# RetNet recurrence and RWKV channel mix on one core: 64-token chunks from block 2 on, four early loads, key weights in quarters, a new order

## The chip, the cores and the metric

The kernel runs on one core of one Trainium2 chip. The metric is the device time of one execution in microseconds, as the median of several runs. A profile of one execution stands beside it; its span runs from the first to the last instruction of the program.

## The reference, cut to what matters

Two layers follow each other. The first is a linear attention with decay (8 heads of 64, 4 sequences of 768 tokens); the second mixes channels (model width 512, hidden width 1024) and looks one token back.

```
state = gamma[h] * state + k_t (outer) v_t          # per head, 64 x 64
y_t   = scale * q_t @ state
x  = y, heads side by side: (4, 768, 512)
xk = mu_k * x + (1 - mu_k) * x_prev;   xr = mu_r * x + (1 - mu_r) * x_prev
k  = relu(xk @ w_k);   v = (k * k) @ w_v;   r = sigmoid(xr @ w_r)
out = r * v
```

## The kernel before, in words

**Blocks.** The 4 x 768 tokens are cut into 12 blocks n = 0..11 of 256 tokens; three blocks make a sequence, and the state is carried from block to block of one sequence. Each block goes through attention pieces and then through three projections (keys, gates, values). GROUPS joins blocks 3 and 4, 6 and 7, 9 and 10 for the keys.

**The order is written out by hand.** ORDER (line 24 on) is a list of words; the kernel is recorded word by word, so each engine runs its own words in exactly this sequence. A word such as `S.6@45` is a code, its block (and further numbers) and the PSUM banks that it uses; `~v`, `~a`, `~p`, `~s` name VectorE (DVE), ScalarE (ACT), GpSimd (POOL) and SyncE (SP). An engine that waits at a word holds back all of its later words. The codes:

- `lq`, `lk`, `lv`: loads of q, k, v of a block (line 222). Most go through GpSimd's queue and turn f32 to f16 on the way for q and k. `wk`, `wr`, `wv`: the weights (lines 733 to 742), on the same queue. `mu`: the two mixing vectors, on ScalarE's queue.
- EARLY (line 18) names loads that land as f32 in a scratch area and are cast by `cq` and `ck` (line 245). Before, these are the first halves (heads 0 to 3) of block 0's q and k, on SyncE's queue.
- `Tq`, `Tk`: transposes on TensorE (line 264); `Eq`, `Ek`: their copies out of PSUM by ScalarE (lines 285, 297). Blocks in WHOLE turn 128 tokens at a time, the others 64.
- `vs`: v times decay (line 252). `S`: scores k by q (lines 312, 324); `M`: the causal mask on their way out of PSUM (line 345). `C`: products of k and v for the state (lines 359, 373), `U`: sums of these into the carried states (line 406), `G`: their decay to the next block (line 421).
- `I`: the part of y that comes from the carried states, for half of the tiles (line 450); `Y`: the part within the chunk, and in most blocks the other half of the carried part (line 470); `J`: that other half alone, where Y lacks it (line 453). `D`: y out of PSUM into x (line 501).
- `dx`, `t`, `X`: the difference to the token before and the two mixes (lines 525, 539, 547); `X.n.0.*` feed the keys, `X.n.1.*` the gates. `K`, `R`, `V`: the projections (lines 567, 608, 622), `Qa` and `Qb` relu and square, `s` the sigmoid, `O` the product, `st` the store.
- `z.c`: matmuls of zeros in spare time (line 700); `mt`, `me`: the mixing vectors turned; `gy`, `cm`: tables made at the start.

**Three kinds of attention.** HALF blocks (6 to 11) cut a block into four chunks of 64 tokens; every matmul is a 64x64 tile with 64 columns, the mask is one instruction of 128x1024, and there are four states to sum (`U.n.0` to `U.n.3`, three in the last block of a sequence). `D` is then two instructions. WIDE blocks (2 to 5) have two chunks of 128 tokens: scores as 64x128 tiles, two masks of 128x1024, two sums (one in the last block of a sequence), one `D`. Blocks 0 and 1 interleave even and odd tokens.

**Start.** constants() (line 662) loads the small tables on ScalarE's queue, clears a few tiles, and applies one Sigmoid to a dummy tile, which makes ScalarE load its function table.

Of the kernel before, what the change touches and what calls it, by code (L numbers as in the profile page):

```python
# [799 lines left out]
```

## Time and profile before

| | |
|---|---|
| median of 3 runs | 153.58 us (153.42 to 153.73) |
| span of the profiled execution | 151.4 us, 2.2 us under that median |
| TensorE (PE) busy | 143.4 us, 2426 matmuls |
| VectorE (DVE) busy | 127.8 us, 212 instructions |
| ScalarE (ACT) busy | 103.6 us, 195 instructions |
| GpSimd (POOL) busy | 55.3 us |
| granted TensorE clock | full throughout |

In a timeline, the columns are the start in us, the time from the start of the first to the end of the last instruction of the merged row, engine, line, operation, tiles (out<-in), shapes and count. Matmuls overlap each other, so what a piece costs on a busy TensorE is read from start to start. PEld is the loading of weights, which runs beside PE. In a group row, "17.9, 577" is the busy time of the group in us and the mean duration of one instruction in ns.

### The profile page before, as it was taken

What the parts mean: (1) busy time and instruction counts of PE and PEld (TensorE: products, weight loads), DVE (VectorE), ACT (ScalarE), POOL (GpSimd) and SP (SyncE); (2) the same over time, 40 slices, a digit from 0 to 9 for tenths busy, and PEclk for the clock granted to TensorE, in tenths of its full rate; (3) what the DMA queues carried; (4) which work ended last, traced back from release to release, by engine and by line L of the source; (5) the groups of instructions that cost most, each with busy time, mean ns of one, the idle gap of its engine ahead of it and who ended that gap; (6) DMA issues with size and microseconds to landing.
All of it is one profiled execution on the core that took longest, in us unless ns stands there. A gap on an engine that the chain in (4) does not pass through costs nothing.

```text
span 151.4 us, 5541 instructions
## 1 busy us (share of the span) xinstructions
PE 143.4 (95%) x2426; PEld 82.8 (55%) x2426; DVE 127.8 (84%) x212; ACT 103.6 (68%) x195; POOL 55.3 (37%) x65
## 2 busy tenths in 40 slices
...
GB/s 140 219 229 197 207 231 192 168 251 212 196 167 202 233 262 107 256 300 198 231 173 126 7 38 283 105 35 45 0 4 0 4 0 211 205 0 0 148 133 139
DMA packets 45624, 22.16 MB, mean 146 GB/s; under 512 B 37400, under 2 KB 41248, under 8 KB 45600
## 3 DMA queue, kind: packets, MB, share of 16 engines
...
q8 instruction: 19, 0.31, 0.8%
q10 hardware_dynamic: 304, 0.18, 0.4%
...
## 4 chain that ended last, share of the span: by engine, by line
PE 73%; DMA 12%; POOL 11%; issue 1%; DVE 0%; POOLq 0%
PE ps L624 27%; PE ps L572 14%; DMA v<-in_v_dram 12%; PE ps L612 12%; PE ps L582 8%; PE ps L278 3%; POOL q L235 3%; POOL k L230 2%; PE ps L441 2%; POOL vs L253 2%; POOL v L230 2%; PE ps L366 1%; PE ps L462 1%; PE ps L642 1%; PE ps L318 1%
## 5 line engine op out<-in xcount | busy, mean ns | idle before, releaser
L624 PE MATMUL ps<-wv,k2s 128*128 128x512 f16 x184 | 44.1, 380 | 0.0
L591 ACT ACTIVATE kr<-ps 128x512 f32<-128x512 f32 x48 | 27.9, 594 | 12.5 <-PE ps L582 6.5
L624 PEld LDWEIGHTS <-k2s 128*128 128x128 f16 x184 | 17.1, 98 | 18.9 <-ACT k2s L603 0.4
L630 DVE SCALAR_TENSOR_TENSOR os<-ps,rs 128x512 f32<-128x512 f32 x23 | 15.6, 684 | 11.9 <-ACT rs L618 9.4
L612 PE MATMUL ps<-wr,xr 128*128 128x512 f16 x96 | 23.5, 379 | 0.0
L582 PE MATMUL ps<-xk,wk 128*128 128x256 f16 x192 | 23.2, 273 | 0.0
L572 PE MATMUL ps<-xk,wk 128*128 128x512 f16 x96 | 23.0, 379 | 0.0
L618 ACT ACTIVATE rs<-ps 128x512 f32<-128x512 f32 x24 | 13.6, 597 | 12.9 <-PE ps L612 12.1
L230 POOL DMA_DIRECT2D k<-in_k_dram x20 | 17.8, 903 | 10.3 <-PE ps L384 6.7
L582 PEld LDWEIGHTS <-wk 128*128 128x128 f16 x192 | 18.1, 98 | 3.7
L241 ACT COPY qT<-ps 128x1024 f16<-128x1024 f16 (+1 forms) x13 | 12.3, 946 | 9.5 <-PE ps L278 7.8
L558 DVE SCALAR_TENSOR_TENSOR xr<-dx,mu,xT 128x256 f16<-128x256 f32 (+1 forms) x32 | 17.9, 577 | 0.1
L230 POOL DMA_DIRECT2D v<-in_v_dram x18 | 16.0, 911 | 3.6 <-DMA wr<-in_moe_w_r_dram 1.9
L558 DVE SCALAR_TENSOR_TENSOR xk<-dx,mu,xT 128x256 f16<-128x256 f32 (+1 forms) x32 | 17.0, 579 | 0.2
L354 DVE TENSOR_TENSOR a<-ps,c_sb 128x1024 f16<-128x1024 f32 (+1 forms) x14 | 14.6, 1066 | 0.9 <-PE ps L339 0.6
L603 ACT ACTIVATE k2s<-kr 128x512 f16<-128x512 f32 x24 | 14.8, 631 | 0.3
L612 PEld LDWEIGHTS <-xr 128*128 128x128 f16 x96 | 9.0, 97 | 10.7 <-issue 0.5
L572 PEld LDWEIGHTS <-wk 128*128 128x128 f16 x96 | 9.1, 98 | 10.5
L599 ACT ACTIVATE k2s<-kr 128x512 f16<-128x512 f32 x24 | 14.5, 627 | 0.3
L241 ACT COPY kT<-ps 128x1024 f16<-128x1024 f16 (+1 forms) x13 | 12.2, 945 | 2.2 <-PE ps L272 1.7
L529 DVE TENSOR_TENSOR dx<-xT 128x1024 f32<-128x1024 f32 x11 | 13.4, 1221 | 0.2
L253 DVE TENSOR_TENSOR vs<-v,csm_sb 128x1024 f16<-128x1024 f32 x10 | 12.2, 1217 | 0.2 <-DMA v<-in_v_dram 0.2
...
## 6 DMA issues: line engine op xcount, KB each, us to landing
out_dram<-os SPq DMA_DIRECT2D x23, 256.0 KB, 2.4
v<-in_v_dram POOLq DMA_DIRECT2D x18, 256.0 KB, 7.7
q<-in_q_dram POOLq DMA_DIRECT2D x11, 256.0 KB, 8.4
...
```

Of the source, the lines that this page charges most:

```text
L230: e.dma_start(out=dst[:, :, i * D : i * D + D], in_=src[:, i * P : i * P + P].rearrange("h p d -> p h d"),)
L241: e.copy(out=out, in_=in_)
L253: e.tensor_tensor(out=VS(n), in0=V32(n).rearrange("p h (i d) -> p i h d", i=2), in1=gks[:, int(half(n) or wide(n)), :, :, None].to_broadca ...
L354: nc.vector.tensor_tensor(out=a_full(n)[:, i, :, j0:j1], in0=pairs(banks("S", n, i, j0))[:, :, j0:j1], in1=(below if wide(n) else causal[: ...
L558: nc.vector.scalar_tensor_tensor(out=XM[w](k)[:, j, t0:t1], in0=DX(k)[:, j, t0:t1], scalar=mu[:, w * NCO + j : w * NCO + j + 1], in1=x[:, ...
L572: nc.tensor.matmul(banks("K", n, g), lhsT=wk16[:, co, g * P : g * P + P], rhs=XM[0](k)[:, co, :], start=(co == 0), stop=(co == NCO - 1),)
L582: nc.tensor.matmul(pz[:, i, :], lhsT=wk16[:, co, fo * P : fo * P + P], rhs=XM[0](k)[:, co, m * TM + t0 : m * TM + t1], start=(i == 0 and c ...
L591: nc.scalar.activation(out=kr, in_=banks("K", n, g, *u), func=AF.Relu)
L603: nc.scalar.activation(out=K2(n)[:, w * g : w * g + w, t0:t1], in_=kr.rearrange("p a t -> p (a t)").rearrange("p (i t) -> p i t", i=w), fu ...
L612: nc.tensor.matmul(banks("R", n, tb), lhsT=XM[1](k)[:, co, t : t + P], rhs=wr16[:, co, :], start=(co == 0), stop=(co == NCO - 1),)
L624: nc.tensor.matmul(banks("V", n, tb), lhsT=K2(n)[:, fo, tb * P : tb * P + P], rhs=wv16[:, fo, :], start=(fo == 0), stop=(fo == NFO - 1),)
L630: nc.vector.scalar_tensor_tensor(out=OS(2 * n + tb), in0=banks("V", n, tb), scalar=1.0 / (KSC * KSC), in1=RS(2 * n + tb), op0=ALU.mult, op ...
```

## The change

The blocks 2 to 5 become HALF blocks, and blocks 2 and 3 leave WHOLE. The second halves of block 0's q and k are loaded as f32 on ScalarE's queue and cast by VectorE (`cq.0.2.4~v`, `ck.0.2.4~v`). The key weights come in four loads of 256 columns. A new piece `w.n~a` (fence) stands behind each `I.n`: ScalarE reads one column per tile of the PSUM banks that I.n wrote, so that Y.n, which writes to the same banks, waits for it. The Sigmoid on the dummy tile becomes a word of its own, `wm~a`, in the middle of block 0's work; in the built program ScalarE has a second table load at that place, beside one ahead of its first cast. The scaling `vs.3` goes from GpSimd to VectorE, and all pieces stand in a new order. What is cut from the two orders below lies behind the first key projection of blocks 6 and 7.

```diff
-HALF = (6, 7, 8, 9, 10, 11)
-EARLY = ((1, 0, 0), (0, 0, 0))
+HALF = (2, 3, 4, 5, 6, 7, 8, 9, 10, 11)
+EARLY = ((0, 0, 0), (1, 0, 0), (0, 0, 2), (1, 0, 2))
-WHOLE = (0, 1, 2, 3)
-WIDE = (2, 3, 4, 5)
+WHOLE = (0, 1)
+WIDE = ()
 ORDER = """
-cm.0~v cm.1~v cm.2~v gy.0~v mu~a lv.0~p lq.0.0.2~s lk.0.0.2~s ck.0.0.2~a cq.0.0.2~a z.12@6
-Tq.0.0.2@0 Tk.0.0.2@1 gy.1~v z.1@2 mt@2 Ek.0.0.2~a Eq.0.0.2~a S.0.1.0.2@01 S.0.0.0.2@45 me~a
-lk.0.2.4~p Tk.0.2.4@3 Ek.0.2.4~a lq.0.2.4~p vs.0~v C.0@67 M.0.1.0.2~v U.0.0~v Tq.0.2.4@2 Eq.0.2.4~a
-lq.1~p lk.1~p z.2@3 S.0.1.2.4@23 U.0.1~v lv.1~p lk.2~p I.0@01 S.0.0.2.4@67 M.0.0.2.4~v wk.0~p
-wk.1~p G.0~a z.2@6 Tq.1@6 Eq.1~a vs.1~p lq.2~p Tk.1@7 Ek.1~a M.0.0.0.2~v M.0.1.2.4~v Y.0 D.0~v
-t.0.0.3~a t.0.0.2~a t.0.0.1~a lv.2~p z.2@4 S.1.1@23 M.1.1~v C.1@01 U.1.0~v z.2@4 I.1@23 S.1.0@67
-X.0.0.1~v t.0.1.2~a X.0.0.2~v Tk.2@0 t.0.1.3~a t.0.0.0~a M.1.0~v X.0.0.0~v z.2@4 Y.1 t.0.1.1~a
-X.0.0.3~v Ek.2~a K.0.0@0 K.0.1@6 lq.4~p U.1.1~v G.1~a wr~p lk.4~p D.1~v dx.1~v X.1.0.2~v X.1.0.0~v
-K.0.2@1 Qa.0.0~a Qb.0.0~a Qa.0.2~a lq.3~p X.1.0.1~v X.1.0.3~v X.1.1.0~v Qa.0.1~a K.0.3@0 Qa.0.3~a
-lk.3~p vs.2~v Tq.2@1 X.1.1.2~v K.1.3@6 K.1.0@0 C.2@7 U.2.0~v lv.3~p Eq.2~a S.2.1@23 M.2.1~v S.2.0@45
-M.2.0~v Qb.0.3~a lv.4~p K.1.1@1 X.1.1.1~v Qa.1.0~a t.0.1.0~a K.1.2@7 I.2@23 Qb.0.1~a Qa.1.1~a wv.0~p
-Qb.0.2~a Tq.4@01 Eq.4~a Y.2 Qa.1.3~a Qb.1.1~a X.0.1.3~v X.1.1.3~v R.1.1@4 Tk.4@01 Ek.4~a J.2 R.1.0@6
-Qa.1.2~a s.1.0~a X.0.1.2~v X.0.1.1~v X.0.1.0~v R.0.1@5 s.0.1~a s.1.1~a R.0.0@7 s.0.0~a S.4.1@01
-Qb.1.0~a D.2~v dx.2~v X.2.0.2~v X.2.0.0~v S.4.0@23 Tq.3@4 Eq.3~a X.2.0.1~v wv.1~p X.2.0.3~v Tk.3@7
-lq.5~p Ek.3~a K.2.2@5 Qa.2.2~a K.2.3@4 M.4.1~v M.4.0~v Qa.2.3~a Qb.2.3~a lk.6~p S.3.1@67 M.3.1~v
-S.3.0@01 vs.3~p C.3@23 U.3.0~a Qb.2.2~a K.2.1@4 Qa.2.1~a K.2.0@2 Qa.2.0~a I.3@45 lq.6~p vs.4~v
-C.4@67 U.3.1~v X.2.1.1~v V.0.1.0@3 M.3.0~v V.1.0.0@2 G.3~a U.4.0~v I.4@01 X.2.1.3~v U.4.1~v J.3
-Qb.1.3~a Y.4 Qb.2.0~a lk.5~p X.2.1.2~v X.2.1.0~v Y.3 D.3~v dx.3~v V.0.0.0@7 V.0.1.1 O.0.1~v Tq.5@45
-J.4 D.4~v dx.4~v R.2.0@6 Qb.2.1~a V.0.0.1 O.0.0~v X.3.0.1~v Eq.5~a Qb.1.2~a V.1.0.1 X.3.0.2~v
-O.1.0~v Tq.6@01 Eq.6~a Tk.6@45 Ek.6~a st.0.0~s lk.7~p st.1.0~s V.1.1.0@3 V.1.1.1 O.1.1~v s.2.0~a
-R.2.1@0 s.2.1~a lv.5~p X.3.0.0~v X.3.0.3~v Tk.7@67 Ek.7~a G.4~a S.6@45 M.6~v Tk.5@23 Ek.5~a vs.5~v
-V.2.0.0@0 K.3.2@1 Qa.3.2~a K.3.0@6 S.5.0@23 M.5.0~v S.5.1@45 C.5@1 U.5.0~v K.3.3@7 Qb.3.2~a Qa.3.0~a
-lq.7~p K.3.7@6 Qa.3.3~a Qa.3.7~a lv.6~p lq.8~p vs.6~v M.5.1~v V.2.0.1 st.0.1~s I.5@67 O.2.0~v
-st.2.0~s C.6@23 U.6.0~a U.6.1~v U.6.2~v K.3.6@1 Qa.3.6~a lk.9~p X.3.1.3~v Y.5 Tq.7@45 Eq.7~a U.6.3~v
-X.3.1.2~v I.6@01 J.5 X.3.1.0~v D.5~v X.3.1.1~v Qb.3.3~a G.6~a V.2.1.0@2 K.3.1@3 V.2.1.1 O.2.1~v
-Qb.3.7~a Qa.3.1~a Qb.3.1~a dx.5~v K.3.4@4 K.3.5@5 Qa.3.5~a X.5.0.0~v X.5.0.3~v R.3.1@2 s.3.1~a
-lv.7~p Qa.3.4~a X.5.0.1~v Qb.3.4~a R.3.0@5 R.4.0@2 s.3.0~a s.4.0~a Qb.3.0~a X.5.0.2~v vs.7~v K.5.2@4
-S.7@67 st.1.1~s M.7~v Qb.3.5~a Y.6 Qb.3.6~a lv.10~p C.7@23 U.7.0~v X.5.1.1~v Qa.5.2~a K.5.0@5
-R.4.1@6 Qa.5.0~a D.6~v s.4.1~a V.4.0.0@4 V.4.0.1 V.3.1.0@5 U.7.1~v Qb.5.0~a X.5.1.3~v U.7.2~v I.7@01
-X.5.1.2~v U.7.3~v Tq.8@67 Eq.8~a X.5.1.0~v O.4.0~v lv.8~p vs.8~v Qb.5.2~a lq.10~p lk.8~p Tk.8@23
-Ek.8~a V.3.1.1 V.3.0.0@4 C.8@67 O.3.1~v st.2.1~s st.3.1~s Y.7 dx.6~v D.7~v Tq.10@23 V.3.0.1 Eq.10~a
-G.7~a dx.7~v X.6.0.2~v V.4.1.0@5 R.5.1@2 s.5.1~a K.5.3@0 Qa.5.3~a R.5.0@2 U.8.0~v O.3.0~v V.4.1.1
-lv.9~p lk.10~p lq.9~p Tk.10@01 s.5.0~a U.8.1~v X.6.0.1~v Ek.10~a X.6.0.0~v Tk.9@23 Ek.9~a K.5.1@7
-Qa.5.1~a X.6.0.3~v K.6.0@4 lq.11~p Qb.5.1~a Qa.6.0~a U.8.2~v I.8@01 vs.9~v S.8@23 M.8~v O.4.1~v
...
+lq.0.0.2~s lk.0.0.2~s cm.1~v cm.0~v lk.0.2.4~a lq.0.2.4~a lv.0~p gy.0~v cq.0.0.2~a z.8@6 Tq.0.0.2@0
+ck.0.0.2~a Tk.0.0.2@1 Eq.0.0.2~a cq.0.2.4~v Ek.0.0.2~a lk.1~p z.2@7 S.0.0.0.2@23 ck.0.2.4~v
+M.0.0.0.2~v lq.1~p Tq.0.2.4@0 S.0.1.0.2@45 lv.1~p vs.0~v M.0.1.0.2~v lq.2~p Tk.0.2.4@1 wk.2~p
+Eq.0.2.4~a Ek.0.2.4~a z.2@7 S.0.1.2.4@67 M.0.1.2.4~v C.0@23 mu~a U.0.0~v Tk.1@0 lk.2~p Ek.1~a
+S.0.0.2.4@45 I.0@67 w.0~a M.0.0.2.4~v gy.1~v Tq.1@1 cm.2~v Eq.1~a Y.0 U.0.1~v G.0~a D.0~v mt@0
+wk.1~p S.1.1@45 M.1.1~v vs.1~p me~a t.0.0.3~a t.0.0.0~a t.0.1.3~a t.0.0.1~a S.1.0@23 t.0.0.2~a z.5@1
+C.1@01 M.1.0~v wm~a U.1.0~v X.0.0.2~v U.1.1~v z.5@7 I.1@67 w.1~a wk.3~p Tk.2@45 X.0.0.1~v t.0.1.0~a
+Tq.2@23 Y.1 Ek.2~a X.0.0.3~v wk.0~p Eq.2~a lv.2~p t.0.1.1~a X.0.0.0~v K.0.1@0 Qa.0.1~a t.0.1.2~a
+D.1~v dx.1~v X.0.1.0~v K.0.2@1 K.0.3@0 K.0.0@2 Qa.0.3~a Qa.0.2~a lk.3~p X.1.0.0~v X.1.0.3~v
+X.1.0.2~v Qb.0.1~a S.2@45 Qa.0.0~a Qb.0.0~a X.1.0.1~v vs.2~v K.1.3@0 G.1~a K.1.1@1 Qa.1.1~a C.2@67
+X.0.1.2~v Qa.1.3~a Qb.1.3~a K.1.0@2 M.2~v Tk.3@45 U.2.0~v U.2.1~v U.2.2~v Ek.3~a K.1.2@3 I.2@01
+X.0.1.3~v w.2~a Qb.0.3~a X.1.1.1~v lq.3~p Qa.1.0~a X.1.1.2~v X.1.1.0~v Qa.1.2~a Tq.3@67 Eq.3~a Y.2
+X.0.1.1~v wr~p R.0.1@4 Qb.1.1~a X.1.1.3~v D.2~v dx.2~v X.2.0.0~v s.0.1~a R.1.0@2 s.1.0~a R.1.1@0
+S.3@67 X.2.0.2~v s.1.1~a X.2.0.3~v lq.4~p Qb.1.2~a Tq.4@45 Eq.4~a R.0.0@1 X.2.0.1~v K.2.1@0 lv.3~p
+vs.3~v s.0.0~a lk.4~p Tk.4@23 C.3@45 U.3.0~a M.3~v Ek.4~a K.2.2@1 Qa.2.2~a K.2.3@6 Qa.2.1~a lv.4~p
+U.3.1~v U.3.2~v I.3@23 w.3~a U.3.3~v G.3~a vs.4~v S.4@45 M.4~v wv.0~p Qb.1.0~a Qa.2.3~a Y.3 Qb.2.2~a
+C.4@01 U.4.0~v U.4.1~v lq.5~p K.2.0@7 Qa.2.0~a wv.1~p U.4.2~v X.2.1.3~v U.4.3~v Qb.2.1~a V.1.1.0@4
+D.3~v X.2.1.0~v X.2.1.1~v V.0.1.0@5 V.1.0.0@0 X.2.1.2~v I.4@67 Tq.5@23 w.4~a Qb.2.0~a Y.4 dx.3~v
+V.0.0.0@1 lk.6~p D.4~v V.1.1.1 Qb.0.2~a V.0.0.1 dx.4~v O.0.0~v X.3.0.3~v Qb.2.3~a G.4~a R.2.1@6
+lk.5~p V.0.1.1 V.1.0.1 O.0.1~v s.2.1~a X.3.0.1~v V.2.1.0@1 X.3.0.2~v Eq.5~a st.0.1~s R.2.0@5 s.2.0~a
+O.1.0~v X.3.0.0~v Tk.5@67 Ek.5~a lv.5~p Tk.6@23 V.2.1.1 vs.5~v O.1.1~v O.2.1~v K.3.0@0 K.3.3@5
+Qa.3.0~a lv.6~p K.3.1@4 X.3.1.3~v Ek.6~a st.2.1~s Qa.3.3~a C.5@67 Qa.3.1~a lk.7~p Qb.3.3~a vs.6~v
+S.5@01 U.5.0~v st.1.0~s Tk.7@23 M.5~v Ek.7~a K.3.5@5 Qa.3.5~a K.3.7@4 Qa.3.7~a U.5.1~v Qb.3.5~a
+lq.7~p K.3.2@2 U.5.2~v X.3.1.1~v C.6@01 U.6.0~a I.5@45 w.5~a lq.6~p Tq.6@67 X.3.1.2~v V.2.0.0@3
+U.6.1~v U.6.2~v U.6.3~v st.0.0~s Eq.6~a Qb.3.1~a X.3.1.0~v Y.5 D.5~v dx.5~v X.5.0.2~v X.5.0.3~v
+Qb.3.0~a Tq.7@67 Eq.7~a X.5.0.0~v lv.8~p K.3.4@0 Qa.3.4~a Qb.3.4~a K.3.6@1 R.4.1@4 V.2.0.1 X.5.0.1~v
+Qa.3.6~a st.1.1~s O.2.0~v s.4.1~a lq.8~p Qa.3.2~a lv.7~p vs.7~v S.6@67 lk.8~p lq.9~p lv.10~p
+Qb.3.2~a Qb.3.6~a M.6~v S.7@01 Tq.8@45 Eq.8~a M.7~v G.6~a R.3.0@2 s.3.0~a K.5.1@3 K.5.3@4 Qa.5.1~a
+Qa.5.3~a K.5.2@5 I.6@67 C.7@23 X.5.1.3~v U.7.0~v U.7.1~v U.7.2~v w.6~a Tk.8@01 Qa.5.2~a Y.6 U.7.3~v
+D.6~v Qb.3.7~a G.7~a R.3.1@4 dx.6~v V.3.1.0@5 R.4.0@2 Ek.8~a vs.8~v V.3.1.1 s.4.0~a s.3.1~a I.7@67
+w.7~a S.8@23 Tq.9@01 Y.7 O.3.1~v V.4.0.0@4 M.8~v K.5.0@5 V.4.0.1 lk.11~p Qb.5.1~a Eq.9~a Qa.5.0~a
+D.7~v Qb.5.3~a Tk.11@01 Ek.11~a lk.9~p lk.10~p dx.7~v X.6.0.3~v X.6.0.0~v X.6.0.2~v Tk.9@23 Ek.9~a
+Qb.5.2~a X.6.0.1~v X.5.1.1~v C.8@67 U.8.0~v V.3.0.0@5 V.4.1.0@0 V.3.0.1 O.3.0~v st.2.0~s lv.9~p
+V.4.1.1 O.4.1~v K.6.6@1 O.4.0~v U.8.1~v K.6.1@2 Qa.6.6~a U.8.2~v Qa.6.1~a K.6.0@0 st.3.0~s K.6.5@1
...
+    fenced = const.tile([P, 2, NJ], F32, name="fenced")
+    warm = const.tile([P, 1], F32, name="warm")
...
+    def fence(e, n):
+        e.copy(out=fenced, in_=pairs(banks("I", n))[:, :, :, 0])
...
-        warm = const.tile([P, 1], F32, name="warm")
         nc.vector.memset(warm, 0.0)
-        nc.scalar.activation(out=warm, in_=warm, func=AF.Sigmoid)
...
+    def warmed(e):
+        e.activation(out=warm, in_=warm, func=AF.Sigmoid)
...
     def load_wk(e, h):
-        f = slice(h * dff // 2, (h + 1) * dff // 2)
+        f = slice(h * dff // 4, (h + 1) * dff // 4)
         nc.gpsimd.dma_start(out=wk16[:, :, f], in_=wks[:, :, f])
```

48 lines of the change are left out of this document (24 added, 24 removed).

## The prediction

> **What bounds the kernel now.** First the page's head and its chain, then the stages.
>
> ```profile
> span 151.4 us, 5541 instructions
> PE 143.4 (95%) x2426; PEld 82.8 (55%) x2426; DVE 127.8 (84%) x212; ACT 103.6 (68%) x195; POOL 55.3 (37%) x65
> PE 73%; DMA 12%; POOL 11%; issue 1%; DVE 0%; POOLq 0%
> ```
>
> PE holds the chain for 73% of the span, and the DMA and POOL shares lie in its early part. The averages hide where the others are full, so I cut the span into stages (columns: length, then busy time of PE, PEld, DVE, ACT, POOL).
>
> ```profile
> 20.00:40.00 20.00, 19.59 (x325) 14.73 (x323) 19.75 (x29) 18.65 (x34) 15.98 (x18) 1.00 1.49 210
> 60.00:86.00 26.00, 26.00 (x535) 14.71 (x536) 25.41 (x42) 19.21 (x36) 13.85 (x16) 1.00 1.30 190
> 120.00:148.00 28.00, 28.00 (x155) 14.89 (x152) 13.97 (x25) 16.91 (x32) 0.00 (x0) 1.00 0.25 94
> ```
>
> From 20 to 86 us PE and DVE are both full (DVE 19.75 of 20, 25.41 of 26), and from 20 to 40 ACT is nearly so (18.65). Only behind 120 us is PE full while DVE is half idle. So an edit that frees PE time early gains only what DVE and ACT can follow. I therefore split the time at two points: `D.1`, from which DVE runs on without a pause, and the first key projection of blocks 6 and 7, which needs DVE's `X.6.0.*`.
>
> ```profile
> 19.78 1.21 DVE L514 TENSOR_TENSOR xT<-ps,gy_sb 128x1024 f32<-128x1024 f32 x1
> 84.38 2.07 DVE L558 SCALAR_TENSOR_TENSOR xk<-dx,mu,xT 128x512 f16<-128x512 f32 x3
> 19.78:86.13 66.35, 65.94 (x1255) 40.22 (x1254) 64.82 (x96) 51.39 (x96) 40.54 (x46) 1.00 1.44 198
> 86.13:148.30 62.17, 62.11 (x858) 33.68 (x855) 46.37 (x75) 40.40 (x76) 0.00 (x0) 1.00 0.23 75
> ```
>
> The first row is `D.1`; the second ends with the last `X.6.0`, beside the start of `K.6.0` at 86.13. Between the two, DVE works 64.82 of 66.35 us; from 86.13 PE works 62.11 of 62.17 us up to its last matmul. What follows to the end of the span (3.1 us) has the same pieces after the change.
>
> **PE's own saving.** Costs are read from start to start.
>
> ```profile
> 33.55 0.62 PE L331 MATMUL ps<-qT,kT 64*128 64x128 f16 x16
> 34.11 0.64 PE L272 MATMUL ps<-c_sb,q 128*64 128x128 f16 x16
> 34.58 0.61 PE L272 MATMUL ps<-c_sb,k 128*64 128x128 f16 x16
> ...
> 42.94 1.08 PE L478 MATMUL ps<-a,vs 128*64 128x128 f16 x32
> 43.95 1.90 PE L624 MATMUL ps<-wv,k2s 128*128 128x512 f16 x8
> ...
> 46.06 0.28 PE L441 MATMUL ps<-qT,tg 64*64 64x128 f16 x8
> 46.28 1.04 PE L612 MATMUL ps<-wr,xr 128*128 128x512 f16 x4
> ```
>
> A wide block's scores take 34.11 - 33.55 = 0.56 us, two `Y` 43.95 - 42.94 = 1.01 (0.50 each), a `J` 0.22, and a transpose of 128 tokens 0.47.
>
> ```profile
> 95.30 0.43 PE L318 MATMUL ps<-qT,kT 64*64 64x64 f16 x32
> 95.55 0.45 PE L278 MATMUL ps<-c_sb,q 64*64 64x64 f16 x32
> ...
> 111.50 0.45 PE L462 MATMUL ps<-a,vs 64*64 64x64 f16 x32
> 111.78 0.32 PE L441 MATMUL ps<-qT,tg 64*64 64x64 f16 x16
> 111.90 0.47 PE L462 MATMUL ps<-a,vs 64*64 64x64 f16 x32
> ```
>
> In 64x64 tiles the scores take 0.25 and a whole `Y` with its carried part 0.40. So four blocks save 4 x 0.31 + 4 x (0.72 - 0.40) = 2.5 us. Block 3's two transposes save about 0.4, and block 2's q transpose moves ahead of the first key projection (0.5).
>
> ```profile
> 82.06 0.87 PE ps L582 x8
> 85.31 0.98 PE ps L582 x8
> ```
>
> The same key piece takes 0.87 us ahead of another projection and 0.98 ahead of small tiles: a change of kind costs 0.1. Counted in the order from the first `K` on, there are 50 such changes before and 44 after: 0.6 us. Together PE has 4.0 us less from the first `K` to the end; nothing it does there is new.
>
> [...]
>
> **DVE's work up to the first key projection of blocks 6 and 7.**
>
> ```profile
> L354 DVE TENSOR_TENSOR a<-ps,c_sb 128x1024 f16<-128x1024 f32 x10 | 12.0, 1219 | 0.3 <-PE ps L331 0.2
> L419 DVE TENSOR_TENSOR tg<-ps,tg 128x256 f16<-128x256 f32 x20 | 8.4, 418 | 0.6 <-ACT tg L424 0.4
> L507 DVE TENSOR_TENSOR xT<-ps,gy_sb 128x512 f32<-128x512 f32 x12 | 8.3, 689 | 0.7
> L514 DVE TENSOR_TENSOR xT<-ps,gy_sb 128x1024 f32<-128x1024 f32 x6 | 7.3, 1218 | 1.4 <-PE ps L441 1.2 <-PE ps L478 0.2
> L253 DVE TENSOR_TENSOR vs<-v,csm_sb 128x1024 f16<-128x1024 f32 x10 | 12.2, 1217 | 0.2 <-DMA v<-in_v_dram 0.2
> L558 DVE SCALAR_TENSOR_TENSOR xr<-dx,mu,xT 128x256 f16<-128x256 f32 x20 | 9.1, 477 | 0.0
> L630 DVE SCALAR_TENSOR_TENSOR os<-ps,rs 128x512 f32<-128x512 f32 x23 | 15.6, 684 | 11.9 <-ACT rs L618 9.4 <-PE ps L624 2.3
> ```
>
> Successive DVE instructions overlap by some 0.08 us (four `X` from 22.28 take 1.68, not 4 x 0.48), so I take 0.08 off each mean.
>
> ```profile
> 22.28 1.68 DVE L558 SCALAR_TENSOR_TENSOR xk<-dx,mu,xT 128x256 f16<-128x256 f32 x4
> ```
>
> Between `D.1` and the last `X.6.0.*` the order after has eight wide masks fewer and five others more (-3 x 1.14), six sums more (+6 x 0.34), `vs.3` from POOL (+1.14), four `D` in two halves (+4 x 0.15), and three `X` and two `O` fewer, which now come later (-3 x 0.40 - 2 x 0.60): -3.4 + 2.0 + 1.1 + 0.6 - 2.4 = -2.1 us. So DVE, which gets 1.4 us lighter by masks and sums and 1.7 heavier by the rest, is not freed; the 2.1 are mostly order. The stretch from `D.1` to the first key piece of blocks 6 and 7 takes 64.3 us if DVE keeps the 1.5 us of idle time of before, 62.8 at best.
>
> PE's rest behind it grows: the two gates of block 5 and two transposes of block 10 come later, three small pieces earlier (2 x 0.86 + 0.54 - 0.8 - two changes of kind 0.2 = +1.3): 63.4 us.
>
> **The start.** `D.1` is the term that carries straight to the end.
>
> ```profile
> 7.54 1.23 DVE L253 TENSOR_TENSOR vs<-v,csm_sb 128x1024 f16<-128x1024 f32 x1 [0.20 <-DMA v<-in_v_dram]
> 13.95 1.23 DVE L514 TENSOR_TENSOR xT<-ps,gy_sb 128x1024 f32<-128x1024 f32 x1 [1.19 <-PE ps L441]
> 15.26 2.90 ACT L542 ACTIVATE dx<-xT,nu 128x256 f32<-128x256 f32 x7 [0.53 <-DVE xT L514]
> k2s<-in_k_dram SPq DMA_DIRECT2D x1, 256.0 KB, 3.5
> L667 ACT ACT_TABLE_LOAD x1 | 1.3, 1283 | 1.2 <-PEq L784 1.2
> L694 ACT COPY mu<-ps 128x8 f32<-128x8 f32 x1 | 0.2, 183 | 0.0
> ```
>
> Before, DVE has `vs.0` and a first mask behind it at 9.4 us and begins `D.0` at 13.95, after 1.19 us of waiting. After, two casts come ahead (never seen on DVE; between nothing and the 0.6 us of other 128x512 instructions; I take 0.45), and 0.5 MB more is loaded beside v. Such a load of 256 KB landed after 3.5 us; two more in a second queue put the last near 6, which `gy.0` on DVE covers; `vs.0` slips 0.3. From 9.7, three masks of half width (3 x 0.62), two sums, `gy.1` and `cm.2` (1.1) bring `D.0` to 13.4, ending near 14.6: 0.5 earlier than before. Two masks, two sums and four `X` (4.6 us) then end at 19.2. `D.1` also needs `Y.1`, and that the new `w.1`, behind five `t` (2.1 of the 2.90 for seven), the table load (1.28) and the dummy Sigmoid (0.2): 14.6 + 2.1 + 1.5 + 0.2 = 18.4, `Y.1` to 19.1. Before, the table load lay ahead of the first load's landing and cost nothing. The quarters of wk keep wk's place in the queue. I take `D.1` at 19.8, as before, from 19.3 (this sum) to 20.9 (mixing vectors, now asked for late, or v landing a microsecond late).
>
> **The fences.** Twelve reads of 128x8, about 0.18 each by the row of L694, add 2.2 us to ACT. For PE a fence is a round trip: between `I.n` and `Y.n` it has 0.3 to 0.7 us of other work in nine of twelve blocks. If ACT is free, the trip costs about 0.4 and is hidden but for 0.1; at worst a `w` stands behind a whole instruction (1.0, a copy of 128x1024). What waits behind `Y.n` is all of PE, then `D.n` on DVE. Up to block 5 PE is ahead of DVE by 1 to 2 us after the change and the wait is covered; I take 0.
>
> **The sum.** 19.8 + 64.3 + 63.4 = 147.5 against 148.3: 0.8 us earlier. The profiled execution would have a span of 150.6, and 2.2 us lie around it: **152.8 us**, a little faster.
>
> **The rivals.**
>
> (a) DVE sheds its idle time, as PE now waits for it and not the reverse: 1.5 us less, 151.3. For it: before, some masks and `D` waited for PE. With PE alone as the bound (4.0 less) it would be 149.6; the DVE row of 60 to 86 us speaks against that.
>
> (b) Late start. `w.1` stands behind the table load on an engine that is now busy; if D.1 comes at 20.9, the time is 153.9. [...]
>
> (c) Slower: the fences decide.
>
> ```profile
> L591 ACT ACTIVATE kr<-ps 128x512 f32<-128x512 f32 x48 | 27.9, 594 | 12.5 <-PE ps L582 6.5
> L241 ACT COPY qT<-ps 128x1024 f16<-128x1024 f16 x11 | 11.1, 1011 | 9.2 <-PE ps L278 7.8 <-PE ps L272 1.4
> ```
>
> Between `w.1` and `w.3` the order gives ACT 20 instructions of 0.5 to 0.6 us (`Qa`, `Qb`, `s`), six copies of 0.9 and some small ones, 19.6 us in all; PE alone would want `w.3` 18.6 us after `w.1`. With the 1.35 us of idle time that ACT had from 20 to 40 it is late by 2.3, against the 1 to 2 by which DVE holds PE back. If then the five later fences with as little cover cost 0.5 each, it is 0.4 + 2.5 = 2.9 more: 155.7. It decides once ACT runs over 1 us behind PE at a `w`.
>
> (d) It does nothing: what PE saves is waited for, DVE's order loses its gain to new waits: 153.6.
>
> **Chances.** Forecast 0.42, (a) 0.14, (b) 0.18, (c) 0.18, (d) 0.08. The range goes from 151.2 to 155.7. A difference under 0.2% (0.3 us) can't be told from none here. Faster takes (a), most of the forecast case: 0.50. Same: 0.17, from the edges of forecast, (b) and (d). Slower: 0.33, from (b) and (c).
>
> **What would show it.** Right: D.1 between 19.3 and 20.3; PE with several waits for DVE between 30 and 85 us, at `K.2`, `K.3` and `K.6`; scores of blocks 2 to 5 at 0.25; few waits for line of `fence`. Wrong: `Y` waiting for ACT in the row of waits with more than 1 us in total; a gap on PE before `Y.1`; DVE idle over 3 us between `D.1` and `X.6.0`; or PE without gaps from 20 us on, which would be (a).

## The result, and the profile after

The kernel after takes 169.8 us (median; 167.8 to 173.0) against 153.5 (153.4 to 153.7), a ratio of 1.103 with a 95% interval from 1.096 to 1.110: slower by a tenth, where 152.8 was forecast. The profiled execution of after is the slowest of its four (173.0 us, span 171.2), so its pauses are somewhat longer than the median's.

First the head of the page of after, its clock row, the row of the queue that brings instructions (packets, MB, share), and its chain.

```profile
span 171.2 us, 6226 instructions
PE 149.8 (88%) x2743; PEld 84.8 (50%) x2743; DVE 129.8 (76%) x223; ACT 105.7 (62%) x208; POOL 53.5 (31%) x64
PEclk9956999996999969999699999999999999999999
q8 instruction: 21, 0.34, 0.8%
PE 66%; DMA 16%; POOL 6%; DVE 5%; issue 4%; ACT 0%; POOLq 0%
```

PE issues 317 matmuls more than before and is busy 6.4 us longer, though its tiles are smaller; its clock row, which had no dent before, has four. "issue", time in which an engine waits for nothing that the profile shows, was 1% of the chain and is 4%. The row of q8 is one that I had read past: 21 packets of 16 KB (16,384 bytes each in the trace's records). PE's 2743 matmuls and 2743 weight loads are 5486 instructions; at 256 to a packet that is 21.4. Before it was 19 packets and 4852 instructions: 19.0.

Then `D.1` in DVE's timeline (start, length, ..., in brackets the idle time before it and what ended it), and in a table by windows the two stages that begin with it.

```profile
26.73 1.23 DVE L516 TENSOR_TENSOR xT<-ps,gy_sb 128x1024 f32<-128x1024 f32 x1 [4.50 <-ACT dx L547]
```

```profile
26.73:103.96 77.23, 66.16 (x1535) 38.45 (x1533) 64.62 (x100) 50.53 (x99) 32.27 (x37) 0.93 1.09 149
103.96:167.80 63.84, 63.64 (x833) 34.38 (x831) 47.84 (x80) 39.89 (x79) 0.00 (x0) 1.00 0.23 78
```

`D.1` comes at 26.73 instead of 19.8, and the stretch to the first key piece of blocks 6 and 7 takes 77.2 us instead of 64.3, in which neither PE (66.2) nor DVE (64.6) is full. Only the rest, 63.8 against 63.4, went as said. Against the trace of before, `D.1` is 7.0 us later, the stretch 10.9 longer and the rest 1.7.

Where PE pauses from 20 us on is seen in its timeline: the first rows behind its six longest pauses (in brackets: length and what ended it).

```profile
24.38 0.31 PE L443 MATMUL ps<-qT,tg 64*64 64x128 f16 x8 [2.18 <-issue]
...
30.06 0.28 PE L587 MATMUL ps<-xk,wk 128*128 128x256 f16 x1 [1.40 <-DVE xk L563]
...
39.67 2.74 PE L617 MATMUL ps<-wr,xr 128*128 128x512 f16 x6 [2.80 <-DMA wv<-in_moe_w_v_dram]
...
51.51 0.45 PE L368 MATMUL ps<-vs,k 64*64 64x64 f16 x32 [1.28 <-DVE a L349]
...
58.74 0.23 PE L464 MATMUL ps<-a,vs 64*64 64x64 f16 x5 [2.27 <-issue]
...
80.02 0.29 PE L280 MATMUL ps<-c_sb,q 64*64 64x64 f16 x13 [1.95 <-issue]
```

The second, and one of 0.90 us right behind it, is an ordinary wait: a key piece needs DVE's `X` of block 0. Two of the other five split a group in the middle: `Y.4` stops after 27 of its 32 matmuls and `Tq.7` after 19. No semaphore stands there. Counting instructions between these five pauses gives the pattern (columns: window, then busy time and, in brackets, number of PE and PEld).

```profile
24.37:36.69 12.32, 9.99 (x256) 8.00 (x256) 9.86 (x18) 8.02 (x18) 8.56 (x11) 1.00 1.48 217
39.65:50.04 10.39, 10.27 (x256) 6.12 (x256) 7.04 (x11) 6.49 (x14) 5.23 (x6) 0.84 1.56 203
51.50:56.29 4.79, 4.77 (x127) 2.95 (x128) 4.02 (x10) 2.28 (x6) 4.79 (x7) 1.00 1.52 202
58.73:77.89 19.16, 19.15 (x384) 9.41 (x384) 16.30 (x25) 10.34 (x17) 1.78 (x2) 0.91 0.77 145
80.01:99.76 19.75, 19.74 (x512) 11.91 (x512) 15.74 (x23) 15.31 (x32) 8.82 (x10) 0.91 0.74 72
```

Between the ends of the pauses lie 512, 512, 255 (one of them at the edge), 768 and 1024 instructions: multiples of 256. **PE pauses where a new packet of instructions begins**, and in after only where it got through the one before in 5 us or less: 256 instructions in 2.30 us ahead of the pause at 36.7, in 2.17 ahead of that at 77.9. In before the borders lie between other pieces, and while loads are under way no 256 instructions pass in less than 5.5 us. Speed alone doesn't decide: in before one block passes in 2.96 us without a pause (102.09 to 105.05), and by the trace its packet had begun at 100.86, ahead of the border. The names that the profile gives to two of the pauses (a load of wv, a mask) are those of the last event before the end of a wait; the gate piece starts without one in two of the experiments (36.77 in a_shift112, 39.91 in a_noload).

The second effect is the clock. The trace's records of it have half clock for 3.41 us or twice that. Four windows of 3.41 us, the first and third with a pause in them (columns as above; the seventh number is the granted clock):

```profile
22.53:25.94 3.41, 1.56 (x21) 1.34 (x21) 0.00 (x0) 1.85 (x4) 3.35 (x5) 1.00 1.96 168
25.95:29.36 3.41, 2.71 (x54) 2.19 (x51) 2.60 (x3) 2.65 (x6) 2.38 (x3) 1.00 1.42 204
77.15:80.56 3.41, 1.46 (x84) 1.02 (x83) 3.24 (x6) 1.62 (x4) 0.00 (x0) 1.00 0.03 5
80.57:83.97 3.40, 3.40 (x10) 1.22 (x8) 2.18 (x5) 2.41 (x4) 0.00 (x0) 0.50 0.02 5
```

Where PE worked 1.46 of 3.41 us, the next 3.41 us have half the clock; where it worked 1.56, they do not. After has such stretches at 39.6, 60.1 and 80.6, each behind a pause at a border, and each takes 1.7 us of full work. A double one from 8.9 on (3.4 us of full work) stands behind no border; it begins within a wait of 2.06 us, up to 9.50, for the second half of block 0's q, and PE idled 2.15 of the 3.41 us ahead of it.

Adding up the PE records of both traces: the last matmul ends at 148.2 before and 167.8 after. Pauses at borders of 256 come to 0.0 and 10.8, all other idle time up to there to 4.9 and 7.1, half clock (its time by two) to 0.0 and 8.5. That is 10.8 + 2.2 + 8.5 = 21.5 more; since the difference is 19.5, PE's work itself fell by some 2.

### The profile page after: what moved, and what is told of

Its sections match the earlier page's. It is cut to its first block, busy times and chain, and to the rows that moved or that the text cites. A ratio compares the mean times of both kernels' runs of the same rounds, so it can differ in the third digit from the quotient of the medians.

```text
span 171.2 us, 6226 instructions
## 1 busy us (share of the span) xinstructions
PE 149.8 (88%) x2743; PEld 84.8 (50%) x2743; DVE 129.8 (76%) x223; ACT 105.7 (62%) x208; POOL 53.5 (31%) x64
## 4 chain that ended last, share of the span: by engine, by line
PE 66%; DMA 16%; POOL 6%; DVE 5%; issue 4%; ACT 0%; POOLq 0%
PE ps L629 23%; PE ps L617 13%; PE ps L577 12%; PE ps L587 7%; DMA v<-in_v_dram 5%; DMA wr<-in_moe_w_r_dram 5%; DMA wv<-in_moe_w_v_dram 5%; PE ps L280 3%; PE ps L368 2%; PE ps L443 2%; PE ps L464 2%; PE ps L320 1%; DVE vs L255 1%; POOL vs L255 1%; POOL v L232 1%
## 5 line engine op out<-in xcount | busy, mean ns | idle before, releaser
L629 PE MATMUL ps<-wv,k2s 128*128 128x512 f16 x184 | 45.6, 389 | 0.0
L617 PE MATMUL ps<-wr,xr 128*128 128x512 f16 x96 | 25.9, 405 | 2.8 <-DMA wv<-in_moe_w_v_dram 2.8
L629 PEld LDWEIGHTS <-k2s 128*128 128x128 f16 x184 | 17.8, 100 | 19.9 <-issue 1.4
L623 ACT ACTIVATE rs<-ps 128x512 f32<-128x512 f32 x24 | 14.1, 594 | 20.5 <-DVE os L635 10.4
L577 PE MATMUL ps<-xk,wk 128*128 128x512 f16 x96 | 24.1, 397 | 0.0
L563 DVE SCALAR_TENSOR_TENSOR xr<-dx,mu,xT 128x256 f16<-128x256 f32 (+1 forms) x32 | 17.2, 577 | 0.0
L617 PEld LDWEIGHTS <-xr 128*128 128x128 f16 x96 | 9.5, 104 | 15.1 <-issue 6.4
L509 DVE TENSOR_TENSOR xT<-ps,gy_sb 128x512 f32<-128x512 f32 x20 | 13.8, 689 | 3.0 <-PE ps L443 1.6
L243 ACT COPY qT<-ps 128x1024 f16<-128x1024 f16 (+1 forms) x13 | 12.3, 946 | 5.4 <-PE ps L274 3.6
L421 DVE TENSOR_TENSOR tg<-ps,tg 128x256 f16<-128x256 f32 x28 | 11.8, 420 | 4.2 <-ACT tg L243 2.1
L349 DVE TENSOR_TENSOR a<-ps,c_sb 128x1024 f16<-128x1024 f32 x10 | 12.1, 1218 | 2.0 <-PE ps L320 1.9
```

What stands on the lines that cost most here:

```text
L243: e.copy(out=out, in_=in_)
L563: nc.vector.scalar_tensor_tensor(out=XM[w](k)[:, j, t0:t1], in0=DX(k)[:, j, t0:t1], scalar=mu[:, w * NCO + j : w * NCO + j + 1], in1=x[:, ...
L577: nc.tensor.matmul(banks("K", n, g), lhsT=wk16[:, co, g * P : g * P + P], rhs=XM[0](k)[:, co, :], start=(co == 0), stop=(co == NCO - 1),)
L617: nc.tensor.matmul(banks("R", n, tb), lhsT=XM[1](k)[:, co, t : t + P], rhs=wr16[:, co, :], start=(co == 0), stop=(co == NCO - 1),)
L623: nc.scalar.activation(out=RS(2 * n + tb), in_=banks("R", n, tb), func=AF.Sigmoid, scale=1.0 / KSC)
L629: nc.tensor.matmul(banks("V", n, tb), lhsT=K2(n)[:, fo, tb * P : tb * P + P], rhs=wv16[:, fo, :], start=(fo == 0), stop=(fo == NFO - 1),)
```

## The experiments

**Theory (blocks):** PE's instructions come in blocks of 256 by DMA; under load a block needs some 6 us from the last one's start (5.9 and 5.1 us in burst, below), and denser code waits and then also loses clock. **Rivals:** the fences; the late start; small tiles that are slow by themselves. The number behind a median is the ratio to before with its interval.

### Moving the borders and nothing else

Tiny matmuls, whose results nobody reads, at the start of PE's work:

```diff
+    def packed(e, count):
+        pz = banks("p", count)
+        z16 = zero.bitcast(F16)
+        for x in range(count):
+            a, u = x % 2, x // 2 % 2
+            nc.tensor.matmul(pz[low(u), a, 0:W], lhsT=z16[low(a), low(u)], rhs=z16[low(a), 0:W], ...)
-... z.12@6 Tq.0.0.2@0
+... z.12@6 p.48@67 Tq.0.0.2@0
```

> The kernel before, with 48 tiny 64x64 matmuls (96 PE instructions, results never read) put in behind the first zero matmuls, while PE waits for the first q. Theory (PE's instructions come in blocks of 256, and under load the next block takes some 6 us from the last one's start): nothing else changes but where the 256-instruction borders fall; the trace of before has stretches in which 256 instructions with the borders moved by 96 pass in less than 6 us, and adding the lacks up over its records gives 5.3 us of waiting instead of 1.0. So 157 to 160 us, with gaps on PE of 1 us or more near 14 and 55 us, at every 256th instruction. Rivals (fences, the late start, small tiles being slow by themselves): none of them is in this kernel and 0.5 us of dummies fit into idle time: 153.5 +- 0.4 us.

Measured: 162.95 us, 1.061 (1.053 to 1.069). The kernel before, with 0.5 us of dummies in an idle moment, loses 9.5 us. PE's timeline of it:

```profile
80.66 0.45 PE L278 MATMUL ps<-c_sb,k 64*64 64x64 f16 x32 [1.28 <-issue]
...
86.31 0.32 PE L278 MATMUL ps<-c_sb,q 64*64 64x64 f16 x16 [2.47 <-issue]
```

and of before, the same transposes:

```profile
76.02 0.45 PE L278 MATMUL ps<-c_sb,k 64*64 64x64 f16 x32
...
78.89 0.47 PE L278 MATMUL ps<-c_sb,q 64*64 64x64 f16 x31
```

No wait before; now 1.28 and 2.47 us, the second in the middle of a group, and 3.4 us of half clock from 86.8. The kind of loss is as expected; its size is over the range, as only the border pauses had been added up, not the half clock (1.7). Their sum, 5.2 us, fits the 5.3 expected by luck in part, as the waits came at 13.7, 36, 79 and 84 us, not at 55. Some 2.6 of the 9.5 us are in neither and weren't taken apart.

> The kernel after, with 56 tiny matmuls (112 PE instructions, never read) behind the first zero matmuls. Theory of instruction blocks: by the same sum the waits at the borders shrink from 12.3 us to 6.5, and one or two of the stretches at half clock that follow them go: 160 to 165 us, 5 to 9 us faster than after, though PE does more. Rivals (fences, start, tiles): all of that is left as it was: 168 to 172 us, as after.

Measured: 165.01 us, 1.074 (1.071 to 1.077); 4.8 us faster than after with more work. Its timeline:

```profile
36.77 2.76 PE L617 MATMUL ps<-wr,xr 128*128 128x512 f16 x12
...
41.98 0.22 PE L280 MATMUL ps<-c_sb,q 64*64 64x64 f16 x4 [1.84 <-issue]
```

The gate piece that in after began at 39.67, "waiting for wv", starts at 36.77 without a wait; the border now lies 256 - 112 = 144 instructions further on, and the pause with it, inside a transpose. And 12 of its matmuls take 2.76 us where, behind the pause, 6 took 2.74: the half clock in one number. The time is as expected, and so are the border pauses, 6.0 us in this profile (6.5 expected, 10.8 in after). The half clock is not: it is 8.5 as in after, where one or two stretches less were expected.

> The kernel after with 116 tiny matmuls (232 PE instructions) at the same place, as the counter-test: the same kind of addition, twice as much of it. Theory of instruction blocks: the sum over the records gives 14.4 us of waits at the borders, 2 more than after: 168 to 174 us. If it were the dummies themselves (a PE kept warm) that help, this one would gain as much as the one with 56.

Measured: 171.64 us, 1.117 (1.112 to 1.123), as the theory has it: twice the dummies, no gain. Its border pauses are 10.4 us, not the 14.4 expected.

Two controls move the borders of before by a whole block (256), so that they fall on the same work.

> The kernel before with 132 tiny matmuls in the place of four of its first zero products: 256 PE instructions more, so every border falls on the same piece of work as in before. Theory of instruction blocks: 153.0 to 154.5 us and no gap of over 0.4 us at a border, though it has nearly three times the dummies of the kernel with 48. Rival (dummies at the start, or the missing zeros, slow it): 157 us or more.

Measured: 157.54 us, 1.027 (1.023 to 1.031). No gap at a border, but the time is the rival's (157 or more), by the second of its two reasons: the edit took four zero products away, the clock became full only at 16.4 us instead of 4.7 (the eight transposes at 10.05 us still take 0.64 us, in before 0.41 from 5.92 on), and `D.0` came 3.0 us late. A control with a fault of its own.

> The kernel before with 128 tiny matmuls (256 PE instructions) behind all of its first zero products, so every border falls on the same piece of work and the clock is full from 4.7 us on. They take 1 us of PE while it waits for q: D.0 up to 1 us later. Theory of the borders' place: 153.3 to 155 us and no gap of over 0.4 us at a border, where the kernel with 48 dummies took 163. Rival (dummies at the start are what costs): 163 us or more.

Measured: 158.60 us, 1.036 (1.030 to 1.042), also above its range and far under the rival's 163; this time by a border. The dummies put the first one at 6.6 us, the packet for the next began only at 11.5, and PE waited for it:

```profile
14.08 0.25 PE L339 MATMUL ps<-qT,kT 64*64 64x128 f16 x3 [2.82 <-issue]
```

From there on the borders lie as in before. `D.0` in this kernel (span 156.7), then in the one with 48 dummies (span 160.4):

```profile
19.22 1.22 DVE L514 TENSOR_TENSOR xT<-ps,gy_sb 128x1024 f32<-128x1024 f32 x1 [2.74 <-PE ps L441]
```

```profile
14.96 1.22 DVE L514 TENSOR_TENSOR xT<-ps,gy_sb 128x1024 f32<-128x1024 f32 x1 [2.34 <-PE ps L441]
```

From `D.0` to the end before takes 151.4 - 13.95 = 137.45 us; shifted by 256, 156.7 - 19.22 = 137.48 (138.5 in the control with missing zeros, `D.0` at 16.99 of 155.5); shifted by 96, 145.44. Same work, same order: the place of the borders, with the half clock behind them, is worth 7 to 8 us.

### The fetch by itself

```diff
-... z.12@6 Tq.0.0.2@0
+... z.12@6 p.512@67 Tq.0.0.2@0
...
-sc.11.1.0~s
+sc.11.1.0~s p.640@23
```

> The kernel before with 512 tiny matmuls of 64x64 (1024 PE instructions) at the start, beside the loads of q, k, v and weights, and 640 (1280 instructions) behind its last product, when no load is under way; none is read. Measures the fetch by itself. Theory: PE stops at every 256th instruction; at the end a block of 256 takes 3 to 4 us from border to border although 128 such matmuls need about 1 us (7.8 ns each in four tiles): some 15 us for 1280 instructions; under load at the start 5 to 6 us a block. Rival (the fetch is hidden): 640 matmuls run through in 5 us without steps, 512 in 4 to 8.

Measured (one execution, 190.1 us). PE's timeline:

```profile
12.62 1.92 PE L721 MATMUL ps<-zero 64*64 64x64 f16 x128 [5.03 <-issue]
18.54 1.93 PE L721 MATMUL ps<-zero 64*64 64x64 f16 x128 [4.00 <-issue]
23.64 0.75 PE L721 MATMUL ps<-zero 64*64 64x64 f16 x39 [3.17 <-issue]
...
174.83 1.62 PE L721 MATMUL ps<-zero 64*64 64x64 f16 x128 [2.49 <-issue]
178.56 1.93 PE L721 MATMUL ps<-zero 64*64 64x64 f16 x128 [2.11 <-issue]
182.29 1.92 PE L721 MATMUL ps<-zero 64*64 64x64 f16 x128 [1.80 <-issue]
```

Rows of exactly 128 matmuls (256 instructions), each behind a pause. With no load under way a block starts 3.73 us after the last one (178.56 - 174.83, 182.29 - 178.56), beside the loads 5.9 and 5.1 us (18.54 - 12.62, 23.64 - 18.54). The rival, a hidden fetch, is out. By the trace's records of the packets, one takes 0.9 to 1.6 us in both places, and PE goes on 1.3 to 1.6 us behind its end; what differs is when it begins: 0.9 to 1.1 us behind the last border at the end, 2.5 to 3.8 beside the loads. The cost of crossing a border is hidden here only for code that takes longer than these times (in before 5.5 to 8.6 us a block beside loads, without a pause), or whose packet began early (100.86 for the border at 105.05 there).

### Less traffic

```diff
-every lq.n, lk.n, lv.n with n from 4 to 11
```

> The kernel after without the loads of q, k and v of blocks 4 to 11: these blocks compute on what blocks 0 to 3 left in the same buffers, every other instruction as in after. With the DMA engines free from some 45 us on, the theory of instruction blocks wants a new block after 3.7 us instead of 6: the border gaps behind 48 us (six us in after, near 50, 56, 78 and 100) fall to under 2 in sum, and the half-clock stretches behind them go: 157 to 164 us. Rivals (fences, order, start): nothing PE waits for there is a load, so 166 to 170 us.

> The control: the kernel before without the loads of q, k and v of blocks 4 to 11 (these compute on what blocks 0 to 3 left). It has no border gaps that could shrink: 152.5 to 153.8 us by both theories; if it gains more than 1 us, loads cost something else too, and that much of the gain of the other kernel without loads isn't the instructions'.

Measured: 163.25 us, 1.067 (1.060 to 1.073), and for the control 154.21, 1.007 (1.004 to 1.009). After gains 6.5 us by it; before gains nothing and loses 0.7%, a little more than expected, which stays unexplained. After without these loads, by windows (instructions under way at the edges are counted in) and in PE's timeline:

```profile
37.48:39.80 2.32, 2.31 (x137) 1.91 (x136) 2.29 (x7) 2.10 (x5) 0.00 (x0) 1.00 0.00 0
```

```profile
39.91 2.45 PE L615 MATMUL ps<-wr,xr 128*128 128x512 f16 x10
```

The 256 instructions ahead of the gate piece again pass in 2.32 us, but no wait follows: their successors' packet had begun at 37.27, just ahead of the border. Behind 37 us the border pauses are 0.8 us in the longest instead of 2.8. Now the rest of the change can be seen without them. `D.1` in after without loads (span 163.0), then in before without (span 152.4):

```profile
29.84 1.22 DVE L514 TENSOR_TENSOR xT<-ps,gy_sb 128x1024 f32<-128x1024 f32 x1 [7.26 <-ACT dx L545]
```

```profile
19.71 1.21 DVE L512 TENSOR_TENSOR xT<-ps,gy_sb 128x1024 f32<-128x1024 f32 x1
```

From `D.1` to the end: 133.2 us against 132.7, where after with its loads takes 171.2 - 26.73 = 144.5. With quick blocks the tiling, fences and order behind the start come out even; what is left of the difference lies ahead of `D.1`, which is 10.1 us later than in the control and 3.1 later than in after (a pause of 4.0 us inside `Y.1`, at a border, is part of it).

### Parts of the change alone

```diff
 (b_half, in before)
-HALF = (6, 7, 8, 9, 10, 11)    WIDE = (2, 3, 4, 5)
+HALF = (2, 3, ..., 11)         WIDE = ()
-S.4.1@01 ... S.4.0@23 ... M.4.1~v M.4.0~v ... I.4@01 U.4.1~v ... J.4
+S.4@01 ... M.4~v ... U.4.1~v U.4.2~v I.4@01 w.4~a U.4.3~v
```

> The kernel before with the tiling of blocks 2 to 5 alone: 64-token chunks in 64x64 tiles with their fences, loads, start, key weights and the rest of the order as before (a second bank for two states, one key piece in another bank). PE issues 2682 matmuls instead of 2426. Theory of instruction blocks: PE's own work falls by some 2 us, but 256 instructions pass faster and the borders move: from the records of before with the new counts the lacks add up to about 7 us more than in before, and a stretch at half clock or two: 158 to 165 us, with gaps at every 256th instruction. Rival (late start): nothing of the start is in here, 151.5 to 154 us. Rival (a small tile costs more than its share): PE's scores of blocks 2 to 5 over 0.4 us each and no gaps at borders.

Measured: 161.69 us, 1.054 (1.050 to 1.058). PE's timeline:

```profile
37.48 0.35 PE L319 MATMUL ps<-qT,kT 64*64 64x64 f16 x20 [1.48 <-issue]
...
40.62 0.45 PE L319 MATMUL ps<-qT,kT 64*64 64x64 f16 x32
40.90 0.40 PE L367 MATMUL ps<-vs,k 64*64 64x64 f16 x28
43.40 0.22 PE L367 MATMUL ps<-vs,k 64*64 64x64 f16 x4 [2.10 <-issue]
```

The scores cost 0.28 us (40.90 - 40.62), so small tiles are not slow by themselves. Of the 8.4 us that this kernel loses (half of the loss of after, without any of its start) two borders are 3.6, where some 7 more than in before were expected, and the half clock from 43.8 is 1.7.

> The kernel before with the tiling of blocks 2 to 5 alone, and without the loads of q, k and v of blocks 4 to 11 (these compute on what blocks 0 to 3 left). Theory of instruction blocks: the gaps at 35.8 and 41.1 us and the half clock behind them shrink from 5.7 us to under 2; what is left against the 154.2 of before without these loads is the fences less PE's saving: 154 to 158 us. Rival (tiling and fences are slow by themselves): 160 to 162.

Measured: 158.19 us, 1.031 (1.027 to 1.034), just over its range: 4.0 us above before without these loads, with 0.65 left at borders. So about half of the 8.4 us stays when the loads go.

> The kernel before with the fences alone: the same ScalarE copy of 128x8 behind the carried products of blocks 1 to 11, its result never read. PE has no instruction more. Theory of instruction blocks: eleven short waits on PE and 2 us on ACT, nothing else: 153.4 to 154.5 us. Rival (the fences make the 16 us): each costs PE a round trip of a microsecond or more, 160 us and up.

Measured: 156.87 us, 1.023 (1.020 to 1.026): dearer than the theory had it, far from the rival's 160. The fence's line in the waits (us in total, times, longest), and PE's timeline:

```profile
ACT fenced L522 <- PE ps L442: 7.8, 6, 1.9
```

```profile
30.13 0.44 PE L279 MATMUL ps<-c_sb,q 64*64 64x64 f16 x30 [1.26 <-ACT kr L595]
...
38.33 0.89 PE L586 MATMUL ps<-xk,wk 128*128 128x256 f16 x5 [1.26 <-DVE xk L562]
```

PE itself waits 0.2 us for a fence; what costs is that ScalarE stands at it: 7.8 us of waiting for PE, and work queued behind it comes late (`D.2` 1.6 us, `D.3` 3.3). The 4.0 us of the tiling without loads are likely of this kind, but that isn't shown: of these eleven fences it has four, at which ScalarE waits 3.4 us for PE and 2.3 for DVE, and its `D.3` is 3.0 us later than in before without loads. In after the order leaves more room: there ScalarE waits 2.5 us at fences and PE 0.3 for them. What they cost there indirectly wasn't measured.

> The kernel after with blocks 2 to 5 in 128-token chunks again (wide scores and sums as before, fences kept), all the rest, the start and the order, as after: 2487 matmuls instead of 2743. DVE gets its four masks and PE 2.5 us back. Theory of instruction blocks: with fewer instructions to a microsecond between 25 and 65 us the waits at the borders shrink by two thirds: 159 to 165 us although both engines do more. Rival (fences, start): nothing of theirs goes, and the tiling was a saving: 170 to 173 us.

Measured: 169.49 us, 1.103 (1.098 to 1.108): missed, by the theory and by the rival. The border pauses did fall from 10.8 to 3.1 us and the half clock from 8.5 to 6.8, but other idle time rose from 7.1 to 12.3; one pause (2.2 us ahead of `Y.3`) is my own, since both scores of block 3 had to share a pair of banks. So 7.7 us less at borders did not make this kernel faster than after: other waits took their place. How much of that is because the order of after isn't made for 128-token chunks can't be told.

> The kernel after with the start undone: second halves of block 0's q and k through GpSimd's queue in f16 behind v as before, no casts for them, the table load first of all; order otherwise as after. Theory of instruction blocks: D.0 comes 1 to 2 us earlier and the wait before Y.1 for the table load goes, but the borders lie where they did and give part of it back: 165 to 169 us. Rival (the late start makes most of the 16 us): D.1, 7 us late in after, comes at 20 us and the time is 160 to 163.

Measured: 168.60 us, 1.098 (1.091 to 1.104): no difference from after that can be told. The time lies in the range expected, but not for the reason given: `D.0` is at 16.39 (16.51 in after), `D.1` at 27.15 (26.73). The second halves on ScalarE's queue and the table load are not what makes the start late.

### The start and the order

```diff
 (a_t, in after)
-t.0.1.1~a X.0.0.0~v K.0.1@0 Qa.0.1~a t.0.1.2~a D.1~v
+t.0.1.1~a t.0.1.2~a X.0.0.0~v K.0.1@0 Qa.0.1~a D.1~v
 (a_warm)    S.0.0.0.2@23  ->  S.0.0.0.2@23 z.7@6
 (a_mend)    gy.0~v  ->  gy.0~v gy.1~v cm.2~v  (taken from behind M.0.0.2.4 and Tq.1);  t.0.1.2 as in a_t;  p.56
 (a_mend2)   as a_mend, z.12 for z.8, z.7 as in a_warm, p.49
```

> The kernel after with one ScalarE instruction moved: t.0.1.2 ahead of Qa.0.1 instead of behind it. In after, D.1 waits for it (4.5 us in the waits, put down to ScalarE), and it waits for Qa.0.1 and so for a key piece of PE. Theory of a false place in the order: D.1 at 24.6 to 25 us instead of 26.7. How much of the 2 us reaches the end tells whether DVE or PE with its borders bounds what follows: 166 to 168 us if DVE does, 168 to 170 (the borders take it back) if PE does.

Measured: `D.1` at 25.05, 1.7 us earlier; time 169.63 us, 1.104 (1.097 to 1.111), as after.

```profile
25.05 1.23 DVE L516 TENSOR_TENSOR xT<-ps,gy_sb 128x1024 f32<-128x1024 f32 x1 [2.39 <-ACT dx L547]
```

The false place in the order is real, but its 1.7 us are given back: the pause at the border near 51 us is 2.93 us here (1.28 in after), and the pause in `Y.1` now has a half clock behind it (25.4 to 28.9).

> The kernel after with zero products (z.7) in PE's pause of 2 us at 7.4. Theory: the pause is what halves PE's clock from 8.9 to 15.7 us; with PE kept busy the clock stays full there, transposes and scores of blocks 0 and 1 take 0.4 instead of 0.64, and D.0 comes 0.5 to 1.5 us earlier; to the end 0 to 2 us, 166 to 170, as the borders move little (10 instructions). Rival: the clock is halved all the same, D.0 at 16.5.

Measured: 168.86 us, 1.102 (1.098 to 1.107). The rival held: a pause of 1.56 us at 5.1 us, waiting for the first k, already has half clock behind it from 7.9 on (0.75 on the mean from 7.91 to 14.73); `D.0` at 16.54.

> The kernel after with gy.1 and cm.2 put ahead of the two casts on DVE (into its wait for q), t.0.1.2 ahead of Qa.0.1, and 56 dummies for the borders. Theory: D.0 at 15 to 15.5 instead of 16.5, D.1 at 23 to 24.5 instead of 26.7; the borders take some of it back: 161 to 165 us, against 165.0 with the dummies alone. Rival (the start decides): 158 to 160.

> The same without the loads of q, k and v of blocks 4 to 11 (these compute on what blocks 0 to 3 left). With blocks every 3.7 us from some 40 us on, the start repaired in part: 155 to 160 us, against 163.25 without the repair. If it comes under 154.2, the change would be worth having on a chip that fetches faster; if it stays at 163, neither the start nor the later borders are what holds it.

> The mended kernel after with z.12 for z.8 and more zeros in PE's pause near 8 us, and 49 dummies, so that the borders lie where they did in a_mend. Theory (the missing zeros halve the clock early): full clock between 9 and 15 us, D.0 at 15 to 15.8 and the time 163 to 165, against 165.6. Rival: the clock stays halved and D.0 at 16.5.

Measured: a_mend 165.58 us, 1.080 (1.076 to 1.084); `D.1` at 24.78, just over the 24.5 expected, `D.0` at 16.70 well over; the time is over its range and no better than with the dummies alone. Without the loads 160.04 us, 1.039 (1.031 to 1.047), 3.2 less than without the repair but not under 154.2. a_mend2 165.82 us, 1.079 (1.073 to 1.085): the clock was full from 9 to 15 us, and `D.0` still late (17.46, a border pause of 1.1 us in `Y.0`). So none of these alone holds `D.0`: neither the loads of the second halves, nor the half clock, nor `gy.1`. The order of block 0's scores, masks and transposes remains and wasn't tried.

No kernel here beat before, and none of the runs points to one that would.

## Why the prediction was wrong

- **What bounds the kernel (wrong, the step that failed).** "From 20 to 86 us PE and DVE are both full", and "an edit that frees PE time early gains only what DVE and ACT can follow". It left out a third bound, the rate at which PE gets instructions. The trace of before has it, in 19 packets of 16 KB, but not as a limit: there 256 instructions take 5.5 to 8.6 us while loads are under way, and PE never stops for them. The stretch forecast at 64.3 us took 77.2; 8.6 us of border pauses (10.8 less the 2.2 in `Y.1`) and three half-clock stretches of 1.7 make 13.7, more than all of the 12.9, and the waits for `X` of block 0 (2.3) come on top; PE's work itself is less there.
- **PE's own saving (right in its prices, wrong in its conclusion).** Scores in small tiles cost 0.27 to 0.28 (forecast 0.25), and PE's work fell by about 2 of the 4.0 us. "Nothing it does there is new" was true piece by piece and false for the stream: in before such bursts of small tiles stood mostly behind 85 us, where the DMA engines move 75 GB/s against 198 before, and between long products. Four more blocks of them put 256 instructions into 2.2 to 4.8 us between 20 and 80.
- **Small tiles.** Their price, 0.25 us for 32 (7.8 ns each), was right for the array; what it leaves out lies one level up: each of them is 64 bytes (16 KB / 256) to be fetched, and the load of its weights another 64.
- **DVE's stage.** DVE works 64.62 us from `D.1` to the first key piece of blocks 6 and 7, not some 62.8, and idles 12.6 us: the sign named for "wrong" (over 3 us). It was not the bound. (The forecast's four `D` in two halves cost 4 x 0.08 by its own overlap of 0.08, not 4 x 0.15.)
- **The start (wrong, the second step that failed).** `D.1` at 26.73 instead of 19.8. The second half of q landed not "near 6" but at 9.0, after 7.2 us, and all of DVE's words behind its cast with it; with PE's wait for that cast (2.06 us) came the half clock from 8.9 to 15.7, for which the sum has no term, and `D.0` came at 16.5 instead of 13.4 (though a_start shows that without this load it would be no earlier). The casts (0.46 and 0.41 against 0.45) and the sum for `w.1` behind the table load (3.8 us from the end of `D.0`, as forecast) were right; the dummy Sigmoid begins at 21.25, straight behind the load (19.96 + 1.28). Not seen was that `D.1` waits for `t.0.1.2` and so for a key piece (1.7 us, a_t), and the border inside `Y.1` (2.2).
- **The rest behind `K.6`: right**, 63.8 against 63.4.
- **The fences.** "I take 0" for PE's own waits fits after (0.3 us). The round trip taken at 0.4 was an estimate; in blocks 2 and 4 of after, where ScalarE is free, it is 0.47 and 0.48 us from the start of the last matmul of `I.n` to `Y.n`. The rival that made them decide named the right way, ScalarE held up, and in before's order they cost 3.5 us. They don't decide: adding them to before leaves 13 of the 16 us unexplained.
- **The rivals.** Late start was named at 153.9, too small by far, since its mechanism (the table load) wasn't the one. None of the four was what happened.

What stays open: why a packet begins later beside loads; which piece of block 0's order makes `D.0` late; what the fences cost in after; and how the 16 us divide exactly, since time saved in one wait can come back in another (a_t, a_wide, a_mend). Only 6.5 of them are shown to go with the loads; the late `D.1` is what stays.
